# Batch 2's first queries and the left ones wait in the first chunk's row space, and the table that orders all work is replaced

## The chip, the core and the metric

The kernel runs on one core of one Trainium2 chip. Five engines with a queue each work side by side: PE (TensorE: matmuls and transposes), DVE (VectorE), ACT (ScalarE), POOL (GpSimd) and SP (SyncE, which here only issues DMAs). An engine takes its instructions in the order in which they were written and waits on semaphores. The metric is the time of one execution in microseconds: 632.9 us, the median of three runs (632.67 to 633.02).

## The reference

For 8 batches and 8 heads, with 576 rows of 64 numbers each:

```
q_s = exp(q - max over the 64);    q_s /= sum over the 64 + 1e-9
k_s = exp(k - max over the rows);  k_s /= sum over the rows + 1e-9
kv  = k_s^T v        (64 x 64 for each head)
x   = q_s kv         (the heads side by side: 4608 rows x 512)
h   = max(x @ w1, x @ w2, x @ w3)      (512 -> 768)
out = h @ w_out                        (768 -> 512)
```

## The kernel before

**Tiling.** A batch is a chunk of 512 rows (the 64 rows that are left of each batch, the "left queries", form a ninth chunk). A pair `n` is two heads of a batch (n = 0 to 3 is batch 0, n = 8 and 9 are the first two pairs of batch 2). Every fp32 matrix is held as a high and a low fp32r part, and a product of two takes three matmuls. For a pair, DVE subtracts, sums and divides, ACT takes the exponentials, PE makes kv (L801) and then x.

**The first stage.** The three first weights come in slices (twelve "joins", `wst` and `wx`, L557 to L587): DVE rounds a slice's high part (L561, L562), combines (L566) and adds (L573) two halves, ACT writes the high part of `wa` (L581) and DVE or POOL the low part (L587, "lo n": slice n). PE multiplies x of chunk 0 by them: the "gate" j,i is block j of 128 hidden columns of weight i, 12 matmuls (L1031) in four steps of three, into one of four banks `pf`. It needs slice 3*(j//2)+i, so j4,i1 needs slice 7. Of the three weights' gates ACT copies the first into `m` (L1044) and DVE takes the maximum with the other two (L1047), which frees the bank; then h is split (L1054).

**The second stage.** From chunk 1 on most products are made in a form with fewer multiplications (seven for eight blocks): it needs sums of x blocks of two chunks (`sums`: "whole" L1621 adds, "less" L1625 subtracts, "high" L1629 on ACT and "low" L1633 on DVE split them) and mixes of weights (`mix_of`: L1171 on DVE or POOL, L1180, L1183). The first product that takes such a sum is P5 of u4 (L1329).

**Queries.** From batch 2 on, the rows of two pairs are loaded together (L687) into one place, `qt2`. Softmax is made there (L850 to L872), and a DVE transpose takes it to `tb` (L877), from which DMAs make qT for PE. The left queries (`left_queries`, L967 to L1010) used the same place. Whoever comes next waits until it is free (room "qt").

**What sets the order.** Every piece of work is a generator that yields steps; a step names its engine, what it waits for (`after`), what it gives, and which rooms it takes and frees. The table `ORDER` (L71 to L153) is a list of 2337 stream numbers: each takes the next step of that stream, so the table is the order of all the queues. A letter behind a number picks the engine where a step may run on two: A is ACT, V DVE, G POOL. A step's cost is only used for how many filler matmuls (L510) PE runs at the start.

Of the kernel before, what the change touches and what calls it, by code (L numbers as in the profile page):

```python
# [8 lines left out]
F32 = mybir.dt.float32  # L9
# [62 lines left out]
2 5 116 116V 116 123 0 115 123V 116 115V 3 116 123 7 19 115 19A 123 123 116V 123V 20 19 19 26 26A 115 1 117 115 26 8  # L72
129 117A 27 129 19G 4 122 122 122 140 115 143 19G 10 130 26 130V 115A 118 141 144 12 137 129 26G 26G 9 143 21 122A 136
130 124 130 6 124V 122 25 130 122 129A 11 129 129 137 118 118 122V 136 18 143 130G 137 32 35 136 125 143A 34 125 22V
315 131 316 23 142 24 137 34V 137V 34 28 29V 136A 143 13 131A 34 30 31 40 42 129A 125 144 125 136 136 136A 34V 143 34V
42V 132 132 138 138A 36 42 317 316 33 144 139 139 37V 318 318 144 42 43 132 144G 139 132 139 14 317 148 151 48 50 50A
147 150 315 150 317 317 42V 315 315 56 155 58 50 145 42V 149 143A 58A 50 38 58 51 44 50V 64 45V 318 145A 150 41 154 58
50V 333 316 316 334 161 318 319 151 333 157 319 319 319 334 158 320 320 164 320 333 59 320 58G 58G 321 321 158G 72
150A 150 321 54 322 62 49 334 52 53V 323 39 163 323 66 66A 60 150 61V 66 322 80 164 55 157 74 74A 74 150A 66 75 74 151
151 164 162 146 74V 322 324 324 46 164A 164 176 164 74V 322 63 67 66V 73 321 82 82A 164A 156 151V 66V 333 82 335 68  # L80
323 323 333V 82 336 157 335 69G 324 324 146 336 96 334 146 165 325 83 326 82V 47 326 98 98A 98 325 325 325 152 157A
326 157 82V 168 152A 153 78 81 327 327 327 99 76 98 157 98V 77V 328 98G 97 153 158 165 165 84 70 71 157A 335 335 158
158 326 336 334G 153 329 329 104 106 158V 106A 85V 335V 165 106 86 15 330 330 100 101V 330 102 103 336 159 159A 106
165V 107 106V 327 337 88 90 90A 90 329 329 313 328 328 328 160 170 331 166 166A 338 106V 91 90 90V 90V 331 110 331 337
167 94 330 338 108 160 109G 167 167 331 313 332 92 336 160 160 332 332 93V 16 17 337 337 337 345 345 332 338 338 177
346 346 177 346 346 169 354 347 345 345 314 178 338 839V 353 839V 839V 178 347 839V 180 178 189 178 347 348 348 348
# [24 lines left out]
386 861G 390 379 250 830 380 861V 861 379 861 861V 861V 391 392 273 380 393 380 380 387 393 393 379 379 379 250 250
380 394 380 397 250 394 394 862 379 379 379 379 250 273 250V 250 380 380 399 398 273G 379 400 380 401 380 380 380 402
# [3 lines left out]
417 378 251 262V 379 262 379 379 284 265 681 681 380 423 419 422 423 380 424 425 380 380 379 379 425 251 340 379 379  # L116
426 262 262 429 426 262 262 262 380 380 380 380 251 251 278 251 407 379 426 430 274 273 379 379 262 262 274 274 285
# [203 lines left out]
def linear_attention_then_maxout_ffn(  # L321
# [40 lines left out]
    QS = S // D  # L362
# [1550 lines left out]
```

## Time and profile before

| | |
|---|---|
| median of three runs | 632.9 us |
| the profiled execution, its own time | 635.14 us |
| its span | 633.4 us |
| TensorE's mean granted clock | 0.991 of full speed |
| busy: PE, DVE, ACT, POOL | 610.4, 473.8, 351.6, 65.6 us |
| mean DMA throughput | 244 GB/s |

A busy time is what an engine's instructions took in all; where it is close to a stretch's length, the engine is full there. An engine's idle time is put down to what ended it. The granted clock is given for each stretch, as a share of 2.4 GHz; a value between a half and one is a mean over time at 1.2 and at 2.4 GHz. A time that begins a row is in us from the start of the span.

### The profile page before, as it was taken

How to read it: one execution, taken by the hardware profiler on the slowest of the kernel's cores; microseconds unless marked ns; L12 is line 12 of the kernel's file. 1: busy time of each engine (PE TensorE's matmuls, PEld its weight loads, DVE VectorE, ACT ScalarE, POOL GpSimd, SP SyncE). 2: the span in 40 equal slices, each digit the busy share in tenths (PEclk: the TensorE clock that was granted, in tenths of full speed). 3: DMA queues.
4: the chain of work that ended last, by engine and by line, in shares of the span. 5: the costliest groups of instructions: out<-in, count | busy, mean ns of one | idle time of the engine just before them, and what ended most of it. 6: DMA issues, size and time to landing. Idle time of an engine off the chain costs nothing.

```text
span 633.4 us, 9769 instructions
## 1 busy us (share of the span) xinstructions
PE 610.4 (96%) x3343; PEld 486.3 (77%) x3343; DVE 473.8 (75%) x684; ACT 351.6 (56%) x878; POOL 65.6 (10%) x55
## 2 busy tenths in 40 slices
PE   6799989999989999999999999999999999999997
PEld 6567768876867787778767877888887788888886
DVE  8999998766989999988377887765538873335572
ACT  5898856453575788575636676412424742223262
POOL 1212302013320132012001000001000000000000
PEclk9999989999979999999999999999999999999999
DMA  8987778679789898998988955788665456676533
GB/s 324 354 310 259 248 276 287 236 239 299 278 280 338 271 327 285 304 325 273 280 284 255 281 179 172 236 249 247 215 211 156 116 157 210 193 225 194 168 98 136
DMA packets 67409, 154.76 MB, mean 244 GB/s; under 512 B 7712, under 2 KB 18592, under 8 KB 63776
## 3 DMA queue, kind: packets, MB, share of 16 engines
q1 hardware_dynamic: 67216, 154.07, 75.0%
q8 instruction: 27, 0.44, 0.3%
q14 instruction: 22, 0.18, 0.1%
q10 hardware_dynamic: 144, 0.07, 0.0%
HBM read 109.28 MB, written 37.75 MB: 232 GB/s over the span
## 4 chain that ended last, share of the span: by engine, by line
PE 55%; DVE 11%; DMA 6%; issue 2%; SPq 1%; ACT 1%; DVEq 0%; ACTq 0%
PE pf L1329 39%; PE pf L1517 14%; DMA ws<-keep_a 3%; DMA bd<-keep_w 1%; DMA keep_s<-mix 1%; PE pa L947 1%; DVE sumf L1621 1%; DVE qt L872 1%; DVE op L1450 1%; PE pa L776 1%; DVE mix L1183 1%; DVE mm L1454 1%; DMA qt<-in_q_rows_dram 1%; SPq L892 1%; DVE mm L1372 1%
## 5 line engine op out<-in xcount | busy, mean ns | idle before, releaser
L1329 PE MATMUL pf<-xb,ws 128*128 128x512 f32 x1134 | 261.3, 390 | 2.0 <-DMA ws<-keep_a 1.7
L1329 PEld LDWEIGHTS pf<-xb,ws 128*128 128x128 f32 x1134 | 212.0, 188 | 48.2 <-DVE qt L872 1.8
L1031 PE MATMUL pf<-x,wa 128*128 128x512 f32 x408 | 103.2, 405 | 4.1 <-DVE m L1047 3.1
L1031 PEld LDWEIGHTS pf<-x,wa 128*128 128x128 f32 x408 | 76.2, 191 | 25.3 <-DVE m L1047 3.5
L1363 DVE TENSOR_TENSOR mm<-pf,mm 128x512 f32<-128x512 f32 x44 | 30.1, 687 | 73.6 <-PE pf L1329 73.4
L1384 ACT COPY pf<-pf 128x512 f32<-128x512 f32 x32 | 18.3, 571 | 92.4 <-PE pf L1329 86.8
L854 ACT ACTIVATE qt<-qt,qm 128x64 f32<-128x64 f32 x180 | 60.1, 337 | 1.6 <-issue 1.6
L1377 ACT COPY u<-pf 128x512 f32<-128x512 f32 x27 | 15.8, 586 | 35.6 <-PE pf L1329 35.4
L854 ACT ACTIVATION_READ_ACCUMULATOR qt<-qt,qm 128x1 f32 x180 | 34.1, 189 | 0.0
L754 POOL PARTITION_ALL_REDUCE kma<-km x12 | 13.5, 1126 | 197.6 <-DVE km L751 149.3
L1454 DVE TENSOR_TENSOR mm<-mm 128x512 f32<-128x512 f32 (+1 forms) x32 | 31.2, 980 | 0.3
L1377 ACT COPY s<-pf 128x512 f32<-128x512 f32 x27 | 15.8, 587 | 21.4 <-PE pf L1329 13.8
L1259 ACT CAST xb<-xf 128x1024 fp32r<-128x1024 f32 x18 | 18.6, 1051 | 13.8 <-DVE xf L1265 7.6
L1517 PE MATMUL pf<-op_a,oh 128*128 128x512 f32 x84 | 25.9, 390 | 0.0
L1517 PE MATMUL pf<-mix,so 128*128 128x512 f32 x84 | 25.0, 396 | 0.0
L1261 DVE TENSOR_TENSOR xb<-xf,xb 128x1024 fp32r<-128x1024 f32 x18 | 21.7, 1216 | 2.1 <-ACT xb L1259 2.1
L1329 PE MATMUL pf<-sum,mix 128*128 128x512 f32 x54 | 16.5, 448 | 2.8 <-ACT sum L1629 1.9
L1517 PEld LDWEIGHTS pf<-mix,so 128*128 128x128 f32 x84 | 15.8, 188 | 3.7
L1542 ACT COPY m<-pf 128x512 f32<-128x512 f32 x16 | 9.4, 586 | 16.4 <-PE pf L1517 16.4
L1369 DVE TENSOR_TENSOR u<-pf,u 128x512 f32<-128x512 f32 x18 | 12.4, 690 | 8.0 <-PE pf L1329 7.9
L761 ACT ACTIVATE kt<-kt 128x1280 f32<-128x1280 f32 x12 | 15.2, 1276 | 5.7 <-DVE kt L756 5.6
L1517 PEld LDWEIGHTS pf<-op_a,oh 128*128 128x128 f32 x84 | 15.7, 188 | 3.3
(234 smaller groups left out, 1128.3 us busy)
## 6 DMA issues: line engine op xcount, KB each, us to landing
ws<-keep_s SPq DMA_DIRECT2D x108, 256.0 KB, 4.1
ws<-keep_a SPq DMA_DIRECT2D x81, 256.0 KB, 3.8
wst<-in_w_dram SPq DMA_DIRECT2D x12, 1024.0 KB, 7.6
keep_a<-wa SPq DMA_DIRECT2D x9, 1024.0 KB, 8.4
so<-keep_t SPq DMA_DIRECT2D x24, 384.0 KB, 4.1
vt<-in_v_rows_dram SPq DMA_DIRECT2D x24, 325.0 KB, 5.5
kt<-in_k_rows_dram SPq DMA_DIRECT2D x12, 640.0 KB, 6.4
keep_s<-mix SPq DMA_DIRECT2D x7, 1024.0 KB, 6.4
```

What stands on the lines that cost most here:

```text
L754: nc.gpsimd.partition_all_reduce(kma, km, P, bass_isa.ReduceOp.max)
L761: nc.scalar.activation(out=kt, in_=kt, func=AF.Exp)
L854: nc.scalar.activation(out=rows3[:, s, :], in_=rows3[:, s, :], func=AF.Exp, bias=qm[:, s : s + 1], accum_out=qs[:, s : s + 1],)
L1031: nc.tensor.matmul(out=ps, lhsT=wa[i][j // 2][:, j % 2, cc, hl], rhs=r, start=(cc == 0 and t == 0), stop=(cc == NC - 1 and t == 2),)
L1259: nc.scalar.copy(out=xb[i][:, 0], in_=src)
L1261: nc.vector.tensor_tensor(out=xb[i][:, 1], in0=src, in1=xb[i][:, 0].bitcast(F32), op=ALU.subtract)
L1329: nc.tensor.matmul(out=bank[on], lhsT=w[:, k, a], rhs=self.operand(p, b, k), start=(i == 0 and p in ("P1", "P5")), stop=(i == 5), skip_gro ...
L1363: nc.vector.tensor_max(out=m, in0=bank[on], in1=m)
L1377: nc.scalar.copy(out=temps()[t], in_=bank[on])
L1384: nc.scalar.copy(out=bank[sb], in_=bank["a"])
L1454: nc.vector.tensor_tensor(out=o[:, parts[k]], in0=x[:, parts[k]], in1=y[:, parts[k]], op=ALU.subtract)
L1517: nc.tensor.matmul(out=bank[on], lhsT=w, rhs=to[k][b][:, kk - k], start=(kk == 0 and i == 0 and not need), stop=(kk == NK - 1 and i == 2), ...
```

## The change

1. Two new places lie in the space of chunk 0's x (`X0_AT`): `qx` for the queries of pairs 8 and 9 and `ql` for the left queries. They are loaded once chunk 0's gates are all done (`("gates", 0)`), and no longer take or free the room "qt". `qt2` is first taken by pairs 10 and 11. The step that makes x of pairs 10 and 11 also waits until the left queries were turned.
2. The whole table `ORDER` is replaced. The same steps run; their order differs, and so do some engine letters. Of work that may run on DVE or POOL, these lists show the part before the second stage's steady state. From POOL to DVE: lo n6 and lo n11, join n0's two adds, h of j1, two "less" (t1, t2). From DVE to POOL: join n3's and n7's adds, one add of n8 and n11, a query step of n0, n2 and n7, one "whole" (r22) and "less" t3. The mixes' L1171 changed places in both directions. PE has 8 filler matmuls fewer (20 for 28).

```diff
 ORDER = """
-2 5 116 116V 116 123 0 115 123V 116 115V 3 116 123 7 19 115 19A 123 123 116V 123V 20 19 19 26 26A 115 1 117 115 26 8
+5 123 123V 0 115 2 116 3 19 115V 4 123 123 116V 123 116 19A 123V 116 20 116 115 115 8 1 19 115 122 122 116G 129 129 9
...
+    qx = place("qx", [P, 2, QS, D], F32, X0_AT)
+    q_left_at = place("ql", [P, H, D], F32, X0_AT + 12288)
...
-                self.qt = qt2[:, self.m]
                 if self.m:
                     return
-                yield Step("S", 0.5, ["clear"], gives=("q", self.n), take=[("qt", self.n)], kb=(128, 4608))
+                early = self.queries() is qx
+                yield Step(
+                    "S", 0.5, [("gates", 0) if early else "clear"], gives=("q", self.n),
+                    take=() if early else [("qt", self.n)], kb=(128, 4608),
+                )
...
+        def queries(self):
+            return qx if self.n < TURNED * NP + 2 else qt2
...
-            yield Step("V", 1.41, ["turn"], take=[("tb", both)], free=[("qt", both)], gives=("tb", n))
+            yield Step("V", 1.41, ["turn"], take=[("tb", both)], free=[("qt", both)] if self.queries() is qt2 else (), gives=("tb", n))
...
-                "T", 1.35, [("bd", n), ("qT", n - 1), *x_free(b)], take=rooms, gives=("xmm", n), free=[("qT", n - 1)],
+                "T", 1.35, [("bd", n), ("qT", n - 1), *x_free(b), "left_turned" if n == TURNED * NP + 3 else None], take=rooms, gives=("xmm", n), free=[("qT", n - 1)],
...
-        yield Step("S", 0.5, ["clear"], take=[("qt", "left")], gives=("q", "left"), kb=(128, 2048))
-        ql = qt2.rearrange("p m s d -> p (m s) d")[:, 0:H, :]
+        yield Step("S", 0.5, [("gates", 0)], gives=("q", "left"), kb=(128, 2048))
+        ql = q_left_at
...
-        yield Step("T", 0.5, take=[*room, ("qT", "left")], free=[("qt", "left")])
+        yield Step("T", 0.5, take=[*room, ("qT", "left")], gives="left_turned")
```

In the changed kernel every line below the new code stands 2 to 8 lines lower, by 8 from the softmax on: L1047 is L1055 there, L1621 is L1629.

The first place is DVE's queue around the maxima of the gates j2 and j3. `wa_83` is the tile of slice 7; the maxima are the rows `m<-pf,m`. Before, the two maxima of row 111 are those of j2,i1 and j3,i1, and row 123 is that of j2,i2:

```order
111 L1047 TENSOR_TENSOR m<-pf,m 128x512 x2
112 L930 TENSOR_TENSOR x_93<-pa,x_91 128x512
113 L826 TENSOR_REDUCE qm_229<-q_201 128x8
114 L573 ISA wx_110<-wst,wx_110 128x1024
115 L561 TENSOR_SCALAR wx_116<-wx_116 128x1024
116 L562 TENSOR_SCALAR wx_116<-wx_116 128x1024
117 L573 ISA wx_110<-wst,wx_110 128x1024
118 L566 SCALAR_TENSOR_TENSOR wx_116<-wst,wx_116 128x1024
119 L806 TENSOR_SCALAR rk<-sm 128x1
120 L807 RECIPROCAL rk<-rk 128x1
121 L573 ISA wx_116<-wst,wx_116 128x1024
122 L587 TENSOR_TENSOR wa_83<-wx_109,wa_83 128x4x2x128
123 L1047 TENSOR_TENSOR m<-pf,m 128x512
```

The same place in the changed kernel: row 100 is the maximum of j2,i1, row 104 holds those of j3,i1, j2,i2 and j3,i2, and row 99 is lo n6 (`wa_80`).

```order
99 L589 TENSOR_TENSOR wa_80<-wx_115,wa_80 128x4x2x128
100 L1055 TENSOR_TENSOR m<-pf,m 128x512
101 L834 TENSOR_REDUCE qm_229<-q_202 128x8
102 L707 TENSOR_REDUCE km_845<-kt 128x1
103 L834 TENSOR_REDUCE qm_231<-q_203 128x8
104 L1055 TENSOR_TENSOR m<-pf,m 128x512 x3
105 L814 TENSOR_SCALAR rk<-sm 128x1
106 L815 RECIPROCAL rk<-rk 128x1
107 L563 TENSOR_SCALAR wx_110<-wx_110 128x1024
108 L564 TENSOR_SCALAR wx_110<-wx_110 128x1024
109 L880 TENSOR_TENSOR qe<-qe,qs_228 128x512
110 L568 SCALAR_TENSOR_TENSOR wx_110<-wst,wx_110 128x1024
```

What moved: eleven rows of other work stood between the maxima of j3,i1 and j2,i2, and now none does; lo n7 (`wa_83`) is row 111 here, behind the maxima.

The second place is PE's queue ahead of its first matmul with slice 7 (gate j4,i1). Before:

```order
184 L1031 MATMUL pf<-x_87,wa_80 128x512
185 L1031 MATMUL pf<-x_89,wa_80 128x512
186 L1031 MATMUL pf<-x_87,wa_80 128x512
187 L1031 MATMUL pf<-x_88,wa_85 128x512
188 L1031 MATMUL pf<-x_90,wa_85 128x512
189 L1031 MATMUL pf<-x_88,wa_85 128x512
190 L1031 MATMUL pf<-x_87,wa_83 128x512
```

The same place in the changed kernel:

```order
189 L1039 MATMUL pf<-x_88,wa_80 128x512
190 L1039 MATMUL pf<-x_90,wa_80 128x512
191 L1039 MATMUL pf<-x_88,wa_80 128x512 x2
192 L1039 MATMUL pf<-x_90,wa_80 128x512
193 L1039 MATMUL pf<-x_88,wa_80 128x512 x2
194 L1039 MATMUL pf<-x_90,wa_80 128x512
195 L1039 MATMUL pf<-x_88,wa_80 128x512
196 L912 MATMUL pa<-ident,qe 128x128 x4
197 L809 MATMUL sm<-vt_191,ke 64x65 x10
198 L1039 MATMUL pf<-x_87,wa_83 128x512
```

What moved: matmuls of the gates j4,i0 and j5,i0 (`wa_80`) that stood behind the first one of slice 7 now stand ahead of it.

The third place is DVE's queue at the sums (`sumf`) for P5. Before:

```order
206 L1621 TENSOR_TENSOR sumf_130<-x_88,x_90 128x1024
207 L1075 TENSOR_TENSOR mm<-pf,mm 128x512 x3
208 L869 TENSOR_SCALAR qs_236<-qs_236 128x18
209 L870 RECIPROCAL qs_236<-qs_236 128x18
210 L872 TENSOR_TENSOR qt<-qt,qs_236 128x1152
211 L877 STREAM_TRANSPOSE tb<-qt 128x2x9x2x32
212 L1075 TENSOR_TENSOR mm<-pf,mm 128x512
213 L1621 TENSOR_TENSOR sumf_131<-x_92,x_94 128x1024
214 L1183 TENSOR_TENSOR mix<-bdf,mix 128x4x128
215 L1625 TENSOR_TENSOR sumf_130<-sumf_130,sumf_129 128x1024
216 L1625 TENSOR_TENSOR sumf_132<-sumf_131,sumf_130 128x1024
```

The same place in the changed kernel; L1629 is "whole", L1633 "less":

```order
200 L1633 TENSOR_TENSOR sumf_131<-sumf_131 128x1024
201 L1191 TENSOR_TENSOR mix<-bd_199,mix 128x4x128 x2
202 L1083 TENSOR_TENSOR mm<-pf,mm 128x512 x3
203 L1179 TENSOR_TENSOR bdf<-bdf 128x2x128
204 L877 TENSOR_SCALAR qs_238<-qs_238 128x18
205 L878 RECIPROCAL qs_238<-qs_238 128x18
206 L1633 TENSOR_TENSOR sumf_132<-sumf_132,sumf_131 128x1024
207 L880 TENSOR_TENSOR qt<-qt,qs_238 128x1152
208 L885 STREAM_TRANSPOSE tb<-qt 128x2x9x2x32
209 L1083 TENSOR_TENSOR mm<-pf,mm 128x512
210 L1629 TENSOR_TENSOR sumf_133<-x_92,x_94 128x1024
211 L1191 TENSOR_TENSOR mix<-bdf,mix 128x4x128
```

What moved: the differences t1 and t2 (rows 200 and 206) came from POOL; the sum r22 (row 206 before) and t3 (row 215 before) went there.

POOL's queue at that place, before:

```order
27 L756 TENSOR_TENSOR kt_1119<-kt_1119,kma 128x1280 [waits PE_49,DMAHW2_49,Activation_49,Pool_49]
28 L1171 TENSOR_TENSOR bdf<-bdf 128x2x128 [waits DMAHW2_49,DMAHW7_49,PE_49,Activation_49]
29 L1171 TENSOR_TENSOR bdf<-bdf 128x2x128 [waits DVE_49]
30 L1625 TENSOR_TENSOR sumf_129<-sumf_129 128x1024 [waits DMAHW1_49,DVE_49,PE_49]
31 L1625 TENSOR_TENSOR sumf_130<-sumf_130,sumf_129 128x1024 [waits DMAHW5_49,DVE_49,Pool_49]
32 L1171 TENSOR_TENSOR bd_197<-bd_197 128x2x128 [waits DMAHW4_49,DVE_49,Activation_49]
```

And in the changed kernel:

```order
24 L1179 TENSOR_TENSOR bd_199<-bd_199 128x2x128 [waits DMAHW4_49,DMAHW6_49,DMAHW1_49,DMAHW7_49,DVE_49,Activation_49]
25 L1629 TENSOR_TENSOR sumf_132<-x_88,x_90 128x1024 [waits DMAHW3_49,DMAHW5_49,DVE_49,PE_49]
26 L1633 TENSOR_TENSOR sumf_132<-sumf_132,sumf_131 128x1024 [waits DVE_49]
27 L1179 TENSOR_TENSOR bd_199<-bd_199 128x2x128 [waits DMAHW2_49,DVE_49,Activation_49]
28 L1179 TENSOR_TENSOR bd_199<-bd_199 128x2x128 [waits Pool_49] x2
```

What moved: POOL has two long instructions there as before, r22 and t3 in place of t1 and t2.

## Rows read from the trace of the kernel before

**Rows 1.** Busy time of PE and DVE in the page's first part.

```profile
PE 610.4 (96%) x3343; PEld 486.3 (77%) x3343; DVE 473.8 (75%) x684; ACT 351.6 (56%) x878; POOL 65.6 (10%) x55
```

**Rows 2.** PE's waits: by whom, us in total, times, longest.

```profile
PE pa L723 <- ACT k L705: 3.2, 1, 3.2
PE pf L1031 <- DVE m L1047: 3.1, 1, 3.1
PE pf L1329 <- ACT sum L1629: 1.9, 1, 1.9
PE pf L1329 <- DMA ws<-keep_a: 1.7, 2, 1.4
PE pf L801 <- ACT ke L736: 1.5, 1, 1.5
PE pf L1329 <- DVE sum L1633: 1.0, 1, 1.0
```

**Rows 3.** Stretches: busy us and instructions by engine, clock, DMA share, GB/s.

```profile
70.00:80.00 10.00, 8.41 (x53) 6.05 (x51) 9.93 (x14) 8.66 (x26) 2.85 (x2) 1.00 0.75 252
80.00:90.00 10.00, 8.12 (x31) 6.53 (x32) 9.86 (x16) 6.62 (x11) 0.14 (x1) 0.83 0.95 375
90.00:130.00 40.00, 40.00 (x251) 32.46 (x249) 31.59 (x55) 21.15 (x58) 5.08 (x4) 1.00 0.64 224
130.00:170.00 40.00, 39.24 (x189) 29.54 (x189) 31.14 (x42) 23.09 (x93) 11.99 (x8) 1.00 0.91 299
170.00:180.00 10.00, 7.17 (x96) 5.46 (x95) 9.49 (x12) 5.44 (x8) 0.00 (x0) 0.89 0.72 217
180.00:190.00 10.00, 10.00 (x36) 7.94 (x35) 7.88 (x17) 6.92 (x31) 4.17 (x5) 0.77 0.88 289
190.00:240.00 50.00, 50.00 (x307) 39.48 (x306) 49.26 (x81) 36.30 (x121) 9.36 (x9) 1.00 0.92 315
310.00:330.00 20.00, 18.56 (x91) 14.17 (x91) 10.99 (x17) 9.00 (x36) 0.00 (x0) 1.00 0.88 282
```

**Rows 4.** DVE in order of time, 67 to 85 us: start, length, instruction.

```profile
67.54 3.43 DVE L566 SCALAR_TENSOR_TENSOR wx<-wst,wx 128x1024 uint32<-128x1024 uint32 x1
70.89 1.27 DVE L1047 TENSOR_TENSOR m<-pf,m 128x512 f32<-128x512 f32 x2
...
75.80 1.22 DVE L566 SCALAR_TENSOR_TENSOR wx<-wst,wx 128x1024 uint32<-128x1024 uint32 x1
...
78.94 2.29 DVE L587 TENSOR_TENSOR wa<-wx,wa 128x1024 fp32r<-128x1024 f32 x1
81.15 0.68 DVE L1047 TENSOR_TENSOR m<-pf,m 128x512 f32<-128x512 f32 x1
...
84.53 1.22 DVE L587 TENSOR_TENSOR wa<-wx,wa 128x1024 fp32r<-128x1024 f32 x1
```

**Rows 5.** POOL in order of time, in the same stretch and at the sums.

```profile
66.93 2.96 POOL L587 TENSOR_TENSOR wa<-wx,wa 128x1024 fp32r<-128x1024 f32 x1 [13.35 <-ACT wa L581]
...
160.79 2.73 POOL L1625 TENSOR_TENSOR sumf<-sumf 128x1024 f32<-128x1024 f32 x1 [3.46 <-DVE sumf L1621]
```

**Rows 6.** DVE in order of time at the sums, 157 to 179 us.

```profile
157.70 1.22 DVE L1621 TENSOR_TENSOR sumf<-x,x 128x1024 f32<-128x1024 f32 x1
...
161.18 3.43 DVE L1621 TENSOR_TENSOR sumf<-x,x 128x1024 f32<-128x1024 f32 x1
...
172.51 2.35 DVE L1625 TENSOR_TENSOR sumf<-sumf,sumf 128x1024 f32<-128x1024 f32 x2
...
175.97 2.36 DVE L1633 TENSOR_TENSOR sum<-sumf,sum 128x1024 fp32r<-128x1024 f32 x2 [0.51 <-ACT sum L1629]
```

**Rows 7.** PE in order of time, the steps around its stalls.

```profile
81.88 5.30 PE L1031 MATMUL pf<-x,wa 128*128 128x512 f32 x15 [3.10 <-DVE m L1047]
...
176.94 0.49 PE L1329 MATMUL pf<-sum,mix 128*128 128x512 f32 x1 [1.88 <-ACT sum L1629]
178.39 5.06 PE L1329 MATMUL pf<-sum,mix 128*128 128x512 f32 x11 [0.95 <-DVE sum L1633]
```

More of the change, by code (lines that the diff above doesn't have):

```diff
@@ L77 @@
[L77 to L86, printed above, removed]
@@ new lines @@
+623V 624V 360 842 361 361 367 843 845V 625V 843 362 362 843V 843V 202 202 360 361 626G 367 206 362 200 362 366 194 366
+313 845V 202 627V 191 202V 202 363 363 363 628G 364 364 364 364 368 363 367 631V 365 365 365 365 844 213 845 845 845V
+633V 313 845V 632 634 629 630 314 847V 635 636 370 205 214 369 201 847G 620 620 639 213 213 847G 620 620 202 201 201
+847G 202 202 236 314 849V 216 637 638 846 640 642 620 228 620 641 620 847 847 847G 214 202 202 643 218 849V 214 847V
+620 849G 644 644 849V 620 225 643 314 647 849 643 849 849V 849V 644 620 620 848 645 648 851V 851V 340 851V 851V 620
@@ new lines @@
+650 649 848 620 851 651 651 652 620 655 652 652 202 202 225 225V 214 225 237 620 620 620 202 656 651 658 203 851 620
+657 313 214 214V 203 314 850 653 649 654 214 224 203 203 313 851V 620 620 853V 851V 853V 217 659 659 620 214 853V 852
+852 214 214 853V 853 660 660 214 620 620 853 663 620 237 237V 226 664 853G 314 812 853V 314 802 813 801 801 812 225
+855G 855G 666 240 620 620 214 665 214 214 214 230 225 225 667 854 242 667 226 226 620 620 668 667 668 620 226 226 857V
+668 226V 226 661 671 620 669 620 620 857G 672 855G 855G 237 249 673 620 674 675 803 803 675 673 203 814 215 215 248
@@ new lines @@
+239 373 261 859G 379 379 379 379 379 379 828 829 822 799 799 799 371 380 830 372 373 837 374 836 372 799 374 254 261
+372 859V 380 374 95 858 375 375 641 381 380 380 829 859 859 837 382 380 376 376 859V 859V 838 241 384 376 377 379 314
+861V 385 646 380 383 386 386 377 239 380 389 379 379 385 379 380 390 377 380 387 861V 861G 379 250 860 861G 861 861
+379 379 379 379 861V 239 861V 380 380 380 392 391 380 393 250 250 380 393 397 379 379 393 379 862 394 394 394 380 380
+395 250 250 250V 379 391 398 380 380 380 400 399 399 379 379 250 380 379 379 379 379 379 401 401 261 402 261 402 380
@@ new lines @@
+380 380 403 379 405 250 379 380 401 402 406 404 681 682 380 380 408 409 380 410 253 262 250 250 379 379 379 250 407
+250 380 413 264 273 379 379 380 380 410 379 379 379 379 262 273 276 380 380 414 380 415 409 416 683 683 417 417 417
+380 418 379 379 250 418 250 681 262 262 418 262 262V 411 380 421 380 285 250 262 379 380 419 380 380 423 423 379 379
+379 379 379 422 380 424 380 379 378 380 251 415 273V 285 425 265 273 426 429 426 285V 380 380 830 379 379 266 251 426
+274 262 379 262 430 380 380 425 427 272 379 425 428 692 692 685 379 379 379 432 687 838 380 433 380 434 273 273 431
@@ L683, in q_load @@
             else:
-                self.qt = qt2[:, self.m]
                 if self.m:
                     return
-                yield Step("S", 0.5, ["clear"], gives=("q", self.n), take=[("qt", self.n)], kb=(128, 4608))
+                early = self.queries() is qx
[3 more added lines that the diff above has]
+                )
                 nc.sync.dma_start(
-                    out=qt2.rearrange("p m s d -> p (m s d)"), in_=q_rows[self.b - TURNED, self.g // 2]
+                    out=self.queries().rearrange("p m s d -> p (m s d)"), in_=q_rows[self.b - TURNED, self.g // 2]
                 )
+        def queries(self):
+            return qx if self.n < TURNED * NP + 2 else qt2
         def k_turned(self):
@@ L847, in q_steps @@
             else:
-                rows3 = qt2.rearrange("p m s d -> p (m s) d")
+                rows3 = self.queries().rearrange("p m s d -> p (m s) d")
                 by_act = ROWS_FROM <= n < ROWS_TO
@@ L875, in q_steps @@
             both = n - self.m
-            yield Step("V", 1.41, ["turn"], take=[("tb", both)], free=[("qt", both)], gives=("tb", n))
+            yield Step("V", 1.41, ["turn"], take=[("tb", both)], free=[("qt", both)] if self.queries() is qt2 else (), gives=("tb", n))
             nc.vector.transpose(
                 out=tb.rearrange("p m e (s c) -> p m s e c", s=QS),
-                in_=qt2.rearrange("p m s (e c) -> p m s e c", e=2),
+                in_=self.queries().rearrange("p m s (e c) -> p m s e c", e=2),
             )
```

82 lines of the change are left out of this document (38 added, 44 removed), and 48 rows, old and new, of the table ORDER.

## The prediction

> **What bounds the kernel now.** I read the page's first part for the busy shares, then PE's waits, then the stretches (for the clock and for engines that are full), and then DVE, POOL and PE in order of time around the two largest losses.
>
> PE is busy 610.4 of 633.4 us [rows 1], so the end moves with the 23 us that PE is idle and with the speed at which it runs, and with little else. The reader should see two things in its waits [rows 2]. The 3.2 and 1.5 us behind ACT belong to the start. Two more losses sit at one instruction each: 3.1 us behind the maximum L1047, at 78.8 to 81.9, and 1.9 + 1.0 us behind the sums L1629 and L1633, at 175 to 178 [rows 2, 7].
>
> Each of these two costs more than its wait. Behind each, the granted clock falls: it is 0.83 in 80 to 90, and 0.89 and 0.77 in 170 to 180 and 180 to 190, with 1.00 in the other stretches shown [rows 3]. At the two levels 1.2 and 2.4 GHz, 0.83 over 10 us is 3.4 us at the lower one; 0.89 and 0.77 are 2.2 + 4.6 = 6.8 us. Time at half speed does half the work, so the falls cost 1.7 and 3.4 us. The two places are thus worth 3.1 + 1.7 = 4.8 us, and 2.8 + 3.4 = 6.2 us.
>
> DVE, not PE, is what they wait for: it is busy 9.93 and 9.86 of 10 us in 70 to 90, and 49.26 of 50 in 190 to 240 [rows 3]. Between them, in 90 to 170, it has 8.4 + 8.9 us free. Part of its time is not its own work: the combine L566 took 3.43 us against 1.22 us eight us later [rows 4] while POOL's lo n6 ran from 66.93 to 69.89 [rows 5], and one of the adds L1621 took 3.43 against 1.22 [rows 6] while POOL ran from 160.79 to 163.52 [rows 5]. Lo n7 took 2.29 against 1.22 [rows 4]. POOL's longer operations hold DVE up by 1.1 to 2.2 us each.
>
> **Term 1, the stall at 78.8.** PE waits for a free bank, so for the maximum of j2,i2, which ran at 81.15. The maximum of j3,i1 ended at 70.89 + 1.27 = 72.16 [rows 4]. The 8.99 us between them hold other work, and in the new order none of it is between them. Lo n6 comes onto DVE ahead, at 1.22 us by the row of another L587 [rows 4], and two or three reduces come ahead as well, some 0.7 each; this leaves over 5 us of advance. Lo n7, which the same gate needs, ended only at 78.94 + 2.29 = 81.23, so it must come earlier too. An estimate over DVE's whole order up to its end, each instruction at the undisturbed duration of its like in the trace, gives 68.6 us of work before and 64.6 after, 4.0 us less. On top come the 2.2 us of stretch that goes with lo n6 on POOL and the 1.1 us in lo n7's own row, 7.3 us in all. PE meanwhile gets matmuls of j4,i0 and j5,i0 ahead of that gate, about 2.2 us more work. Against a wait of 3.1 us that is ample: wait and half clock go, which is -4.8. I leave 0.5 us for a new small wait (half of the 1.0 us of [rows 2]) and take -4.3. Bounds: -4.8 and 0. What is late next would be the split of h or x for chunk 1, and DVE's 8.4 free us in 90 to 130 cover them.
>
> **Term 2, the start.** PE's waits of 3.2 and 1.5 us behind ACT [rows 2] stand in a stretch in which ACT, DVE and POOL all get a new order. DVE's first part of x comes about 3 us of work earlier, but the trace cannot show which wait ACT then sets. Bounds: -3.2 (the longest wait) and +1.5 (the other one doubled). I take -1.0, nearer to nothing than to the gain. The eight fillers cost nothing either way; they ran inside the waits.
>
> **Term 3, the sums.** From the first "whole" at 157.70 to the end of the second "low" at 175.97 + 2.36 = 178.33 [rows 6] DVE took 20.6 us, while POOL did t1 and t2. Now DVE does t1 and t2, 2.35 us by the row of two such subtractions [rows 6], and gives r22 (1.22) and t3 (half of 2.35) to POOL; with a mix and a query step that changed sides, its own work between the two points goes from 16.9 to 17.6 us by the same kind of estimate, +0.7. What it may lose is the stretch: 20.6 holds 2.2 us for the add at 161.18. If r22 and t3 on POOL meet DVE no worse than half as often, t1's low part comes about 2 us earlier, and of 2.83 us of wait 0.8 is left. A wait of 1.4 us behind a weight load left the clock at 1.00 in 310 to 330 [rows 2, 3], so one of 0.8 should as well, and 3.4 go too. That is -5.4 if it turns out so, and about -1 if the stretch stays; I take -3.5. Bounds: -6.2, and +8.5 (the third rival).
>
> The Trainium skill, "SBUF — State Buffer", section "Who interferes with whom", says that a DVE instruction with two SBUF inputs contends with a GpSimd one that reads SBUF, and that the order of issue, not the shape, decides who blocks, for the whole instruction. The trace agrees: the add that began at 161.18 ended at 164.61, 1.1 us behind POOL's end at 163.52. By that rule the change could also work against itself: t1 and t2 on DVE stand exactly where r22 and t3 hold POOL's port. With the rule at its worst term 3 is the third rival's; without it, -5.4.
>
> **Term 4, given back.** In 190 to 240 DVE has 0.74 us free in 50 and DMA's share is 0.92 [rows 3], and PE waits 1.7 us for weight loads (`ws`) in 300 to 320 [rows 2]. A PE that arrives earlier finds DVE as full as before and the loads little earlier. Bounds: 0 and +6 (all that terms 2 and 3 gain, and the wait for weights doubled). I take +2.0.
>
> **Term 5, the queries.** The loads wait for chunk 0's gates rather than for a cleared place, and behind them on SP stand other loads and stores of this time. No wait of PE for a query's DMA stands in its waits [rows 2]. Nothing is taken; if a weight load behind them comes late, the price is bounded by one more wait like the 1.7 us for `ws`. The new wait of pairs 10 and 11 for the left queries is covered: those were loaded last before and are now among the first. Freeing `qt2` lets query work move into DVE's free time in 90 to 170; that is in term 3's count.
>
> **Sum.** -4.3 - 1.0 - 3.5 + 2.0 = -6.8. The profiled execution took 635.14 us (1.74 beyond its span), 2.24 more than the median of the runs. 635.14 - 6.8 = 628.3; on the runs' scale 632.9 - 6.8 = **626.1 us**.
>
> **Rivals.**
>
> *All of it.* Both falls of the clock go and nothing is given back: 632.9 - 4.8 - 1.0 - 6.2 = 620.9. For it speaks that from 90 to 170 DVE has time; against it that DVE and DMA are full right after. Chance 0.12.
>
> *Only the first place, and the second stage takes it back.* DVE's work at the sums is 0.7 us more, the port's losses stay, the clock falls again, and DVE and the weights give little way up to 320: term 3 is 0 and term 4 is 2 to 6, so 632.9 - 4.3 - 1.0 + 2 to 6 = 629.6 to 633.6. Chance 0.15, of which 0.05 is no change.
>
> *POOL holds the port at the sums.* Three of DVE's adds meet r22, t3 and a mix where one met t1: two more times 2.2 us, and 0.7 of work, make t1's low part 5.1 us later. The half clock then lasts as much longer as it did for the 2.83 us here, +3.4: term 3 is +8.5. 632.9 - 4.3 - 1.0 + 8.5 + 2.0 = 638.1. It decides once term 3 is above +3.3. For it speaks that POOL takes over a sum that the next steps need at once; against it that POOL's list at that place is no longer than before. Chance 0.2 for this and the slower side around it.
>
> **How the numbers follow.** Forecast 0.53, with 621.5 to 629 as its own range; all of it 0.12; second rival 0.15; third 0.20. A measurement of this kernel tells about 0.2%, or 1.3 us, from no change. Faster: 0.53 + 0.12 + 0.10 = 0.75; the same 0.05; slower 0.20. The range leaves out a tenth on each side: the full gain with term 2 at its bound (618.7) and what lies beyond, and the third rival's upper part: 618.5 to 637.
>
> **What would show it.** Term 1: no wait for L1055 (L1047 before) above 1 us, and a clock of 1.00 in 70 to 90. Term 2: the sum of PE's waits before 60. Term 3: P5's wait behind the sums below 1 us and a clock of 1.00 in 165 to 190; one near 0.8 there means the second or third rival. In DVE's order of time the adds at the sums should take 1.2 us each. Term 4: PE's waits between 190 and 330 grow from about 2 to some 4 us. The prediction is wrong if the first clock fall stays, or if new waits above 1 us stand before 150, since I expect none there.

## The result, and the profile after

The changed kernel takes 614.88 us (median of 4 runs, 614.24 to 615.31), the old one 632.78 in the same comparison: a ratio of 0.9716, interval 0.9699 to 0.9733. That is 17.9 us faster, below the predicted range. The sign was right; the size was forecast at 6.8.

PE's busy time in the page of the new kernel, against [rows 1]: 10.0 us less, in a span 20.9 us shorter.

```profile
PE 600.4 (98%) x3327; PEld 483.5 (79%) x3327; DVE 465.7 (76%) x684; ACT 353.2 (58%) x880; POOL 63.6 (10%) x53
```

PE's waits in the new kernel, us in total, times, longest (lines are 8 higher in number than in [rows 2]):

```profile
PE pa L731 <- ACT kt L713: 1.3, 1, 1.3
PE pa L731 <- ACT k L713: 1.3, 1, 1.3
PE pf L1337 <- DVE sum L1641: 0.5, 1, 0.5
...
PE pf L1039 <- DVE m L1055: 0.2, 1, 0.2
PE pf L1039 <- DVE wa L589: 0.2, 1, 0.2
```

The 3.1 us behind the maxima are 0.2, the 2.9 behind the sums 0.5, and no wait for weights (`ws`) of 0.2 us or more is left.

The new kernel's stretches, columns as in [rows 3]:

```profile
70.00:80.00 10.00, 10.00 (x65) 8.04 (x64) 9.86 (x14) 9.77 (x22) 2.09 (x1) 1.00 0.90 321
80.00:90.00 10.00, 10.00 (x46) 7.58 (x45) 9.49 (x18) 7.81 (x20) 1.05 (x1) 1.00 0.80 233
90.00:130.00 40.00, 40.00 (x262) 32.09 (x262) 37.60 (x62) 27.95 (x96) 4.94 (x4) 1.00 0.89 313
130.00:170.00 40.00, 39.45 (x252) 31.46 (x251) 36.29 (x56) 24.21 (x73) 12.25 (x8) 1.00 0.95 319
170.00:180.00 10.00, 10.00 (x45) 8.25 (x44) 9.76 (x21) 6.08 (x25) 1.82 (x2) 1.00 0.99 350
180.00:190.00 10.00, 10.00 (x55) 7.49 (x54) 9.76 (x15) 6.33 (x20) 2.15 (x2) 1.00 0.84 326
190.00:240.00 50.00, 50.00 (x341) 39.50 (x340) 48.47 (x74) 40.71 (x123) 13.90 (x11) 1.00 0.91 295
310.00:330.00 20.00, 20.00 (x134) 15.76 (x132) 11.09 (x18) 11.14 (x47) 2.12 (x1) 1.00 0.89 290
```

The clock is 1.00 in each, where [rows 3] had 0.83, 0.89 and 0.77. Between 90 and 130 DVE works 37.6 of 40 us (31.6 before) and DMA's share is 0.89 (0.64 before): both do work there that came later before.

DVE at the first place (compare [rows 4]): lo n6 at 64.01, the four maxima, lo n7 at 72.94, each at its undisturbed length.

```profile
64.01 1.22 DVE L589 TENSOR_TENSOR wa<-wx,wa 128x1024 fp32r<-128x1024 f32 x1
65.14 0.68 DVE L1055 TENSOR_TENSOR m<-pf,m 128x512 f32<-128x512 f32 x1
...
67.59 1.87 DVE L1055 TENSOR_TENSOR m<-pf,m 128x512 f32<-128x512 f32 x3
...
72.94 1.22 DVE L589 TENSOR_TENSOR wa<-wx,wa 128x1024 fp32r<-128x1024 f32 x1
```

DVE at the sums (compare [rows 6]), two "whole", then t2, r21, and two "low":

```profile
145.12 2.36 DVE L1629 TENSOR_TENSOR sumf<-x,x 128x1024 f32<-128x1024 f32 x2 [0.41 <-PE pf L1039]
...
153.01 1.16 DVE L1633 TENSOR_TENSOR sumf<-sumf,sumf 128x1024 f32<-128x1024 f32 x1
...
157.35 1.45 DVE L1629 TENSOR_TENSOR sumf<-x,x 128x1024 f32<-128x1024 f32 x1
...
161.79 2.36 DVE L1641 TENSOR_TENSOR sum<-sumf,sum 128x1024 fp32r<-128x1024 f32 x2 [0.56 <-ACT sum L1637]
```

POOL at the sums (compare [rows 5]), r22 and t3:

```profile
149.93 2.49 POOL L1629 TENSOR_TENSOR sumf<-x,x 128x1024 f32<-128x1024 f32 x1 [9.02 <-PE pf L1039]
...
154.25 3.46 POOL L1633 TENSOR_TENSOR sumf<-sumf,sumf 128x1024 f32<-128x1024 f32 x1 [1.83 <-DVE sumf L1633]
```

From the first "whole" to the end of the second "low" it is 19.0 us, 20.6 before. Here it is POOL's t3 that is stretched: 3.46 us, against 2.42 for a like subtraction on POOL in the old kernel (its t2):

```profile
164.73 2.42 POOL L1625 TENSOR_TENSOR sumf<-sumf,sumf 128x1024 f32<-128x1024 f32 x1 [1.21 <-issue]
```

DVE's sums are hardly stretched (1.45 once).

**Where the time came from.** For each PE step I took its start and subtracted the work that stands ahead of it in that kernel's own order, each kind of step at its median distance to the next where PE did not wait. What remains is what PE had lost by then, all in one: waits, half clock, the filler matmuls, and steps that follow each other at more than their median distance. The columns say by how much the new order lost less, in a pair of executions (the two profiles shown) and in a second pair (e13, which has every queue in the old order, and e15, the changed kernel again).

| PE's work done | old time | forecast | lost, old and new | pair 1 | pair 2 |
|---|---|---|---|---|---|
| 0 to 54 us (the start) | to 78 | 1.0 | 24.4, 19.7 | 4.7 | 6.0 |
| 54 to 65 (first stall) | to 95 | 4.3 | 5.5, 0.7 | 4.8 | 3.8 |
| 65 to 140 | to 174 | none | 3.7, 1.5 | 2.2 | 1.2 |
| 140 to 150 (sums) | to 190 | 3.5 | 6.5, 1.2 | 5.2 | 3.9 |
| from 150 | to the end | -2.0 | 8.0, 4.0 | 4.0 | 3.1 |
| all | | 6.8 | 48.0, 27.2 | 20.8 | 18.0 |

The profiled execution of the old kernel is 2.4 us longer than its median, and pair 1 shows more than the medians' 17.9 for that reason; pair 2 fits them. The pairs differ in the clock: at the start e13 is 6.8 us at the lower level and e15 3.4, the two profiled kernels none; at the sums the old kernel is 6.8 us there and e13 3.4, the new ones none.

### The profile page after: what moved, and what is told of

It is laid out like the page before. It is cut to its first block, busy times and chain, and to the rows that moved or that the text cites. A ratio compares the mean times of both kernels' runs of the same rounds, so it can differ in the third digit from the quotient of the medians.

```text
span 612.5 us, 9732 instructions
## 1 busy us (share of the span) xinstructions
PE 600.4 (98%) x3327; PEld 483.5 (79%) x3327; DVE 465.7 (76%) x684; ACT 353.2 (58%) x880; POOL 63.6 (10%) x53
## 4 chain that ended last, share of the span: by engine, by line
PE 88%; DVE 9%; issue 1%; DMA 1%; ACT 0%; SPq 0%; DVEq 0%; ACTq 0%
PE pf L1337 50%; PE pf L1525 19%; PE pf L1039 10%; PE pf L1112 3%; PE pa L955 2%; PE pa L784 2%; DVE wa L589 1%; DVE wx L568 1%; DMA q<-in_q_first_dram 1%; DVE wx L563 1%; DVE wx L564 1%; DVE wx L575 1%; DVE sumf L1629 1%; PE pa L927 1%; DVE km L707 0%
## 5 line engine op out<-in xcount | busy, mean ns | idle before, releaser
L1039 PE MATMUL pf<-x,wa 128*128 128x512 f32 x408 | 100.0, 399 | 0.4 <-DVE m L1055 0.2
L862 ACT ACTIVATE qt<-qt,qm 128x64 f32<-128x64 f32 x162 | 54.1, 340 | 3.7 <-DVE qm L858 3.4
L862 ACT ACTIVATION_READ_ACCUMULATOR qt<-qt,qm 128x1 f32 x162 | 31.1, 192 | 0.0
L1462 DVE TENSOR_TENSOR mm<-mm 128x512 f32<-128x512 f32 (+1 forms) x32 | 30.1, 952 | 0.1
L762 POOL PARTITION_ALL_REDUCE kma<-km x12 | 15.5, 1290 | 121.6 <-DVE km L759 81.6
L1368 ACT COPY mm<-pf 128x512 f32<-128x512 f32 x20 | 11.8, 588 | 13.4 <-PE pf L1337 13.3
L969 ACT COPY xf<-pa 128x512 f32<-128x512 f32 x20 | 11.2, 589 | 13.7 <-PE pa L955 13.7
```

Source lines behind the costliest of these rows:

```text
L762: nc.gpsimd.partition_all_reduce(kma, km, P, bass_isa.ReduceOp.max)
L862: nc.scalar.activation(out=rows3[:, s, :], in_=rows3[:, s, :], func=AF.Exp, bias=qm[:, s : s + 1], accum_out=qs[:, s : s + 1],)
L1039: nc.tensor.matmul(out=ps, lhsT=wa[i][j // 2][:, j % 2, cc, hl], rhs=r, start=(cc == 0 and t == 0), stop=(cc == NC - 1 and t == 2),)
L1462: nc.vector.tensor_tensor(out=o[:, parts[k]], in0=x[:, parts[k]], in1=y[:, parts[k]], op=ALU.subtract)
```

## The experiments

In the mixed tables (e1 to e4, e11, e14) a step whose place or input was not there yet was put off until it was.

**e13 and e1: the places alone.** e13 has the changed kernel's code with the old table; only the step of no engine that reports "chunk 0's gates are done" is listed earlier, so every engine's queue is the old one.

```diff
 # e13: the changed kernel
 ORDER = """
-5 123 123V 0 115 2 116 3 ...      (the new table)
+339 2 5 116 116V 116 123 0 ...    (339: the gates' report; then the old table)
```

> The changed kernel's code with the old table exactly: every engine's queue stands in the old order, only the two places and their waits are new (in e1 the loads of pairs 8 and 9 and of the left queries had slipped behind later steps). Theory, the places alone change nothing, since no queue moves: within 1.5 us of the old kernel. Rival, the earlier load of the left queries and the free qt2 shorten the losses between 100 and 160 us: 2 to 4 us faster.

Measured: 633.2 us, ratio 0.9997 (0.9978 to 1.0015). The theory held. SP's waits between 90 and 135 us show what took the place of the freed one. In the old kernel the left queries' load stood 12.9 us at SP's head for its place, and all the loads behind it too:

```profile
SPq L972 <- DVE tb L877: 12.9, 1, 12.9
```

In e13 that wait is gone, and a load of k that stands behind it waits for its own place instead:

```profile
SPq L654 <- PE pa L783: 12.2, 2, 11.9
```

e1 was meant for the same and failed as a test: there the report came late, so the new loads slipped behind later steps of SP.

```diff
 # e1: the changed kernel, the old table without that early report
-5 123 123V 0 115 2 116 3 ...
+2 5 116 116V 116 123 0 ...
```

> The changed kernel's code (queries of pairs 8 and 9 and the left ones in chunk 0's x) with the old table; only about 10 steps per engine stand elsewhere, since the loads now come after chunk 0's gates. Theory, the table does nearly all of it: within 1.5 us of the old kernel (632.8), and PE keeps a wait of about 3 us behind the maximum L1055 and about 3 us behind the sums. Rival, the free place by itself lets query work run earlier: 3 us or more faster, above all in the losses after 90 us.

Measured: 657.7 us (1.0372, 1.0342 to 1.0402), with a wait of 16.1 us at the left queries' transposes. It says only how dear a late query load is.

**e2: the table without the places.**

```diff
 # e2: the old kernel
-2 5 116 116V 116 123 0 ...
+5 123 123V 0 115 2 116 3 ...
```

> The old code (one place for all queries from batch 2 on) with the new table; a step whose place is not yet free is put off until it is, which moves 8 steps on DVE, 2 on ACT and 3 on SP. Theory, the table does nearly all of it: 615 to 617 us. Rival, the places carry the second stage (the queries of pairs 10 and 11 then come late and x of chunk 2 is late): 618 to 625 us, with a new wait of PE at x of pairs 10 and 11 between 125 and 145 us.

Measured: 634.6 us (1.0015, 0.9989 to 1.0042). Neither theory nor rival: nothing at all is left of the gain. One wait of PE, at the left queries' transposes, takes it:

```profile
PE pa L990 <- DVE qt L985: 15.5, 1, 15.5
```

By the count above e2 loses 18.4 us there (wait and half clock; 0.79 granted in 90 to 130), and from 95 us of work on 5.8 us, the same as the new kernel (5.9). So places and table are worth nothing alone and 17.9 us together; as I read it, the table asks for the queries at a time at which one place cannot have them.

**e3 and e4: front and rest.** P holds the steps that the new table lists before chunk 1's first gate.

```diff
 # e3: the changed kernel;  P = the first 407 steps of the new table
-ORDER = P (new order), others (new order)
+ORDER = P (old order and letters), others (new order)
 # e4
+ORDER = P (new order), others (old order and letters)
```

> The changed kernel with the steps that its table lists before chunk 1's first gate (407 of 2337) in their old order and with their old engines; the rest keeps the new order. Theory, the losses of front and rest add up: the front's 9.4 us are lost and the rest's 11 us stay, so about 624 us (621 to 627). Rival A, the rest only gains because the front's work is done earlier: near 632. Rival B, the front's gain is eaten later anyway, as term 4 of the prediction had it: near 616.

Measured: 624.0 us (0.9843, 0.9808 to 0.9878), as the theory had it. After the front e3 has lost 30.3 us (old 30.1, new 20.8), and from there to the end 6.4, exactly as the new kernel. PE comes to the second stage 9.6 us later than in the new kernel and loses neither more nor less there. The weights' wait is gone in e3 too.

> The reverse: those 407 steps in the new order, all the others in the old one. Theory, the losses add up: the front's 9.4 us are kept and the rest's are lost, about 623.5 us (621 to 627), PE again waits about 3 us behind the sums and 1 to 2 us for weights (ws) near 300 us. Rival B (term 4 of the prediction): DVE and the weight loads take part of the front's gain back, 627 to 631 us, with waits for ws well above 2 us.

Measured: 636.4 us (1.0039, 1.002 to 1.0058), the opposite of the theory. PE's waits:

```profile
PE pa L783 <- ACT kt L768: 4.3, 1, 4.3
...
PE pf L1111 <- ACT m L1075: 2.9, 1, 2.9
PE pf L1336 <- ACT sum L1636: 2.1, 1, 2.1
PE pf L1336 <- DMA ws<-keep_a: 1.4, 1, 1.4
```

The first two lie at the seam (between 100 and 120 us), where the one table leaves undone what the other takes as done; they and a clock of 0.83 cost 12.9 us. Behind the seam, from 95 us of work on, e4 loses 16.4 us, the old kernel 17.8 and the new one 5.9. So the front's gain was lost in the seam: PE comes out of it no earlier than in the old kernel, and e4 cannot say whether the old rest would have taken that gain back.

**e5, e9 and e12: who adds at the start.**

```diff
 # e5: the old kernel, join n0's adds (L573)
-... 129 19G 4 122 122 122 140 115 143 19G 10 ...
+... 129 19V 4 122 122 122 140 115 143 19V 10 ...
```

> The old kernel, but join n0's two adds (L573) run on DVE instead of POOL; nothing else moves. They stand behind the two clamps L561/L562 that took 3.38 us in all while POOL added. Theory, the start's 3.2 us wait of PE behind ACT L705 goes back to DVE (the maxima of k, L699, begin at 16.72 behind those clamps): the clamps take 1.4 us, the wait falls to about 1.3 to 2 us, total 1 to 2 us faster. Rival, ACT or k's DMA (landed 13.1 to 13.9) sets it: the wait stays near 3 us and the time at 632.8.

Measured: 631.3 us, ratio 0.9959 (0.9939 to 0.998), 2.6 us by the ratio. Theory: PE's wait at the start is 1.0 us, where [rows 2] had 3.2, and the first stall is untouched.

```profile
PE pf L1030 <- DVE m L1046: 3.3, 1, 3.3
...
PE pa L722 <- ACT k L704: 1.0, 1, 1.0
```

In e5 and in e9 below, the kernel's own count also puts in six filler matmuls more, and two in e12.

```diff
 # e12: the changed kernel, the same two steps of stream 19
-19V ... 19V
+19G ... 19G
```

> The changed kernel with join n0's two adds back on POOL. Theory, the reverse of the same edit on the old kernel: the clamps that follow on DVE are stretched while POOL adds, and 1 to 2.5 us are lost before 30 us: 616 to 617.5. Rival, in the new order the maxima of k stand ahead of those clamps, so nothing on PE's path waits: within 0.7 us of 614.9.

Measured: 614.7 us (0.9715, 0.9681 to 0.9749). The rival: in the new order the same letters cost nothing, and nothing is lost against e15's 616.2 either. The clamps are held up there too (1.67 and 1.42 us, from 17.9 to 21.1), but the maxima of k, which ACT needs, stand ahead of them, at 12.74.

```diff
 # e9: the old kernel, letters of the new table
-19G ... 19G ... 69G ... 98G ... 334G ... 625G ... 626V ... 627G ... 628V
+19V ... 19V ... 69V ... 98V ... 334V ... 625V ... 626G ... 627V ... 628G
```

> The old kernel with only engine letters changed, as the new table has them: join n0's adds, lo n6, the add of join n10, the split of h of j1, t1 and t2 on DVE; r22 and t3 on POOL. Places and order stay old. Theory, the letters are worth about a third: the start's and the first stall's waits shrink as they did with those letters alone, the sums gain 0 to 2 us, 628 to 631. Rival, letters without the order only move the waits: within 1.5 us of the old kernel. Other rival, the letters are most of the change: under 624.

Measured: 631.9 us (0.9972, 0.9955 to 0.9989), 1.8 us. All the letters give no more than the two of e5. Nearest is the first rival, though its bound of 1.5 us is just passed: the waits move. In the old order the sums now wait longer, not shorter:

```profile
PE pf L1328 <- ACT sum L1628: 3.4, 1, 3.4
PE pf L1030 <- DVE m L1046: 2.7, 2, 1.9
```

**e6 and e7: the first stall.**

```diff
 # e6: the old kernel;  lo n6, the add of join n10, the split of h of j1
-69G ... 98G ... 334G
+69V ... 98V ... 334V
```

> The old kernel, but POOL's three operations between 60 and 82 us (lo n6, an add of join n10, the split of h of j1) run on DVE; the order stays. DVE gets 2.4 us more work and loses 4.4 us of stretch. Theory, the port is half of the first stall: PE's wait behind L1047 falls from 3.1 to about 1.1 us, and the clock in 80 to 90 stays at 1.00, so 3 to 4 us faster. Rival, the wait stays above 2.5 us because DVE simply has more to do: within 1.5 us of the old kernel.

Measured: 632.6 us (0.9987, 0.9966 to 1.0009). Its traced wait at the first stall is 0.6 us, where [rows 2] had 3.1, and that stretch loses 1.6 us of 5.5, as the theory had it. But 1.5 us are lost right after, with a new wait of 1.1 behind the maximum L1046 at 97 us, and 1.2 more later, with one behind ACT at 159 us, so the time does not show it. The clock in 80 to 90 is 1.00; it is also 1.00 in e3, e7 and e10, where lo n6 is on POOL as before, so that is no evidence for the port.

```profile
PE pf L1030 <- DVE m L1046: 0.6, 1, 0.6
...
80.00:90.00 10.00, 9.42 (x41) 7.18 (x41) 9.86 (x17) 8.81 (x17) 0.00 (x0) 1.00 0.95 372
```

```diff
 # e7: the old kernel;  335, 336: the maxima of j2 and j3
-335 (j2,i1) 336 (j3,i1) ... (lo n7) 335 (j2,i2) ... 336 (j3,i2)
+335 (j2,i1) 336 (j3,i1) ... 335 (j2,i2) ... (lo n7) ... 336 (j3,i2)
```

> The old kernel, but the maxima of j2,i2 and j3,i2 stand right behind that of j3,i1 (as in the new table); all else stays. Theory, lo n7 sets the gate j4,i1 just as late: PE waits about 3 to 4 us, now behind lo n7 (L587), the clock falls again, no gain (within 1.5 us of the old kernel, or slightly slower). Rival, the bank alone was what PE waited for (the prediction's wording): the wait goes below 1 us and 3 to 5 us are gained.

Measured: 634.1 us (1.0006, 0.9988 to 1.0024): no gain, as expected, and the gate waits for slice 7 instead. The edit did less than its expectation says: the maximum of j2,i2 came ahead of lo n7 (76.71 us), that of j3,i2 did not (84.33). The wait for slice 7 is shorter than expected, since a wait for ACT came ahead of it; e10, which leaves this place as it was, has the same 2.1 behind ACT and then 1.4 behind the maximum L1046. So the wait was handed over whole.

```profile
PE pf L1030 <- ACT m L1043: 2.3, 2, 2.1
...
PE pf L1030 <- DVE wa L586: 1.4, 1, 1.4
```

**e8 and e15: the port at the sums.**

```diff
 # e8: the changed kernel;  t1, r22, t2, t3
-625V ... 626G ... 627V ... 628G
+625G ... 626V ... 627G ... 628V
```

> The changed kernel, but at the sums t1 and t2 go back to POOL and r22 and t3 back to DVE; positions in the table stay new. Theory, who takes the port is half of term 3: DVE's adds are stretched again by 2 us or more, PE waits 1.5 to 3 us behind the sums (0.5 in the changed kernel), with or without a fall of the clock: 1 to 6 us slower than 614.9. Rival, the earlier query work alone made room: PE's wait stays below 1 us and the time within 1.2 us of 614.9.

Measured: 618.8 us (0.9773, 0.9739 to 0.9807), 3.9 us above 614.9 and 2.6 above e15's 616.2, with intervals that just overlap. In the profiled execution, the fastest of the four (the others have a mean clock of 0.994 to 0.997 and take 1.8 to 3.5 us more), the sums lose 3.4 us (140 to 150 of work), 2.2 more than in the new kernel, and the clock stays at 1.00.

```profile
PE pf L1335 <- ACT sum L1635: 1.5, 1, 1.5
...
PE pf L1335 <- DVE sum L1639: 1.0, 1, 1.0
```

DVE's adds there take 1.2 us each; what is stretched while POOL does t1 is a pair of mixes (1.28 in the new kernel):

```profile
147.78 3.49 DVE L1189 TENSOR_TENSOR mix<-bd,mix 128x512 fp32r<-128x512 f32 x2
...
147.66 2.46 POOL L1631 TENSOR_TENSOR sumf<-sumf 128x1024 f32<-128x1024 f32 x1 [6.12 <-DMA vt<-in_v_rows_dram]
```

```diff
 # e15: the changed kernel, no edit
```

> The changed kernel itself again, beside the same runs of the old one, as the mark for e8, e11, e12 and e14: 614 to 616 us; PE's waits behind the sums 0.5 us in all, and none for weights. A theory that the sums' wait is chance would see 2 us there in this run.

Measured: 616.2 us (0.9726, 0.9706 to 0.9747), a little above the range given. The short wait at the sums held:

```profile
PE pf L1337 <- DVE sum L1641: 0.5, 1, 0.5
```

**e10, e11 and e14: the late stage.**

```diff
 # e10: the old kernel, SP's queue
-v(25) ... ws25 ws26 q(22) ws27 ws28 v(24) ws29 ... ws34
+... ws25 ws26 ws27 ws28 ws29 ... ws34 v(25) q(22) v(24)
```

> The old kernel; only SP's queue differs: three loads (v of pairs 24 and 25, q of pairs 22 and 23, 1.2 MB) that stand among the weight loads at 294 to 300 us stand six weight loads later. Theory, PE's wait for weights is what else stands in the DMA queue at that place: the wait of 1.4 to 1.7 us between 300 and 325 falls below 0.5; time 1 to 2 us less. Rival (term 4 of the prediction), DMA is full over the whole stretch, so a wait of the same size stays, at most some us later.

Measured: 643.8 us (1.0175, 1.0138 to 1.0212). The wait for weights did go, but DVE then stood waiting for the loads that were put off, and PE behind it:

```profile
PE pf L1328 <- DVE mm L1368: 9.4, 1, 9.4
```

So these loads were not early at all, and the edit answers less than it should: PE came 9.4 us late to the weights, so that the wait for them went need not be due to the order of the loads.

```diff
 # e11: the changed kernel, SP's queue
-ws20 ... ws45 of chunk 3 with what stands between (new order)
+the same steps, with v(24) and v(25), in their old order
```

> The changed kernel with some 40 steps of SP's queue (weight loads of the second stage around 275 to 310 us, and the copies and loads between them) in their old order; 13 steps move on SP, 6 on DVE, 3 on ACT. Theory, a wait for weights of 1 to 2 us comes back near 290 us, 616 to 617 us. Rival, the new kernel is ahead with its loads anyway: no wait above 0.5 us, time as the changed kernel's.

Measured: 624.9 us (0.9855, 0.9818 to 0.9891), 8.6 slower than e15's 616.2, and not by a wait for weights but behind ACT:

```profile
PE pf L1335 <- ACT pf L1390: 4.5, 1, 4.5
```

Its profiled execution was 4.7 us longer than its median, and six DVE and three ACT steps moved with the thirteen of SP; so no more is read from it than that the order there is worth several us.

```diff
 # e14: the changed kernel;  P = the first 1000 steps of the new table
-ORDER = P (new order), others (new order)
+ORDER = P (new order), others (old order and letters)
```

> The changed kernel, its first 1000 steps (to about 230 us) in the new order, all later ones in the old one. Theory, what the first term 4 got wrong lies in the order of the late steps: about 3 us come back as PE waits between 240 and 320 (behind ACT L1384 and the weight loads), 617 to 619 us. Rival, the late stage runs well because the early one leaves the loads ahead: below 616 us and no wait for weights above 0.5 us.

Measured: 626.8 us (0.9891, 0.9871 to 0.991). Again a seam, a wait of 6.5 us behind DVE near 250 us, hides what was asked; behind it (260 to 300 of PE's work) e14 loses 1.5 us, old 3.0, new 0.5. What the late order alone is worth stays open.

## Why the prediction was wrong, step by step

**Term 1 (-4.3) was right.** The two pairs show 4.8 and 3.8. Of its two causes, e6 shows that the port's part takes most of the wait (0.6 us is left of 3.1), e7 that one maximum moved alone only hands it to lo n7; the place in full was not run alone. Its 1.7 us for the clock hang on the execution: with POOL's part as before the clock in 80 to 90 was 0.83 in the old kernel, e5 and e13, and 1.00 in e3, e7 and e10.

**Term 2 (-1.0) was too small:** 4.7 and 6.0. The prediction stopped at ACT, who ended the wait. One step further back in the trace stood DVE's two clamps, stretched while POOL added (3.4 us in all; undisturbed they take 0.68 and 0.69, at 10.4 and 11.1 us), and behind them the maxima of k that ACT waited for:

```profile
13.24 3.01 POOL L573 TENSOR_TENSOR wx<-wx,wst 128x512 int32<-128x512 int32 x2 [11.94 <-ACT ke L736]
...
13.38 1.72 DVE L561 TENSOR_SCALAR wx<-wx 128x1024 f32<-128x1024 f32 x1
15.13 1.67 DVE L562 TENSOR_SCALAR wx<-wx 128x1024 uint32<-128x1024 uint32 x1
16.72 1.40 DVE L699 TENSOR_REDUCE km<-k 128x1 f32<-128x576 f32 x2
...
17.50 1.55 ACT L705 ACTIVATE k<-k,km 128x640 f32<-128x640 f32 x2 [2.72 <-DVE km L699]
```

e5 gives 2.6 us for the two letters alone; the new order gets past the clamps in another way (e12). A part could not be seen in one profile: between 10 and 30 us the old kernel's profiled execution keeps the clock at 1.00, while the six other traces with the old order and letters there (e1, e3, e6, e7, e10, e13) are 3.4 or 6.8 us at the lower level; of the eight traces with the new order there only e4 and e15 fall, by 3.4.

```profile
20.00:30.00 10.00, 9.88 (x79) 7.66 (x79) 8.83 (x20) 8.84 (x29) 3.92 (x3) 0.70 0.81 306
```

That row is e13's.

**A term is missing.** In 65 to 140 of PE's work the new order loses 2.2 and 1.2 us less. The clock is 1.00 there in both kernels, and PE's idle time in 90 to 170 is 0.8 us before [rows 3] and 0.55 after, so most of it is no traced wait: PE's steps follow each other more closely, and why stays open. The prediction saw DVE's 17 free us in 90 to 170 and named query work that could move into them, but put that into term 3's count and gave the stretch no term; DVE's busy time and DMA's share in 90 to 130 did rise, which does not show that this made the difference.

**Term 3 (-3.5) was right in kind and too small:** 5.2 and 3.9. It weighed the port by half; e8 shows that who takes these sums is worth 2.2 us of the trace and 2.6 to 3.9 in time. The pairs differ by the clock, which the old kernel lost for 6.8 us and e13 for 3.4: without that part (3.4 and 1.7 us of work) they show 1.8 and 2.2, about what the traced waits fell by (2.83 to 0.5). The term took one execution's falls as the kernel's. The Trainium skill's rule ("SBUF — State Buffer", "Who interferes with whom") was weighed as a rival against the change; the trace agrees that both engines can lose, and in the new kernel it was POOL's t3 that was held, 3.46 us for 2.42, not DVE. e9 is the same letters in the old order, where the sums' longest wait is 3.4 us.

**Term 4 (+2.0) had the wrong sign:** -4.0 and -3.1, and this is the step that failed most. It said that a PE that arrives earlier finds DVE as full and the loads little earlier. For the new order e3 refutes it: with PE 9.6 us later at the second stage, the new rest loses the same 6.4 us, so nothing that the front gained is given back. For the old order it stays untested (e4). Of the 4.0 us, 2.0 are waits of PE that the new kernel lacks, 1.7 for weights and 0.3 behind ACT; the rest shows in no wait. SP's waits show one reason why a gain is kept, first in the old kernel, then in the new:

```profile
SPq L1296 <- PE pf L1329: 124.7, 138, 3.0
```

```profile
SPq L1304 <- PE pf L1337: 125.6, 138, 4.2
```

138 weight loads wait for PE to give back a place. They come earlier when PE does. DVE waits for PE likewise in the second stage, here in the old kernel:

```profile
DVE mm L1363 <- PE pf L1329: 73.4, 26, 5.9
```

So the two engines that were to take the gain back are themselves released by PE there. Which change of order took the waits of 300 to 320 away is not settled (e10, e11 and e14 did not isolate it).

**Term 5 (0) was wrong as it stood.** It went by PE's waits, and no query's DMA stands among them. The loss was at SP: 12.9 us at the head of its queue. Alone the place frees nothing (e13): a load of k behind it then waits as well, 11.9 us; but without the place the new table loses 18.4 us (e2).

In sum: of the 11.1 us between forecast and median, term 4 is 5 to 6, term 2 is 4 to 5, and the missing term and term 3 are 2 to 4; pair 1's own excess of 2.4 over the medians and term 1 make the rest.

## What to carry to other kernels

Before booking that a gain is given back later, ask what releases the engine that would take it back: one that waits for PE's places moves along with PE. Follow a wait back past the engine that ended it, and read the waits of the engine that issues the DMAs too: an idle stretch of DMA or DVE next to a long wait at the head of a queue is room that another order can use. A new place and a new order can be worth nothing alone and everything together, so test both alone before naming either as the cause. Do not book a fall of the clock that one execution shows as a fixed cost: look at several.

## What the runs showed that I had not expected

The table mixed from two good orders is worse than either: 12.9 us at one seam (e4), and 6.5 (e14). The same two letters are worth 2.6 us in one order (e5) and nothing in another (e12). And like waits at the sums leave the clock at either level. In the old order PE waits 1.8 or 1.9 us there and then 0.7 to 1.0, and the clock in 170 to 180 and 180 to 190 was 0.89 and 0.77 in the old kernel [rows 3], 0.88 and 0.78 in e7, 0.86 and 0.97 in e5, 0.94 and 0.89 in e6, 0.98 and 0.85 in e13, but 1.00 in both in e10:

```profile
170.00:180.00 10.00, 7.25 (x99) 5.40 (x98) 9.46 (x13) 5.67 (x9) 0.00 (x0) 1.00 0.73 230
180.00:190.00 10.00, 9.62 (x43) 7.51 (x42) 9.83 (x20) 8.55 (x38) 4.52 (x5) 1.00 0.96 304
```

Over all its executions on record the old kernel's mean granted clock runs from 0.986 to 0.997, and its time from 631.2 to 636.7 us.
